# Pairing heads across two groups so that landmark products run in 64-row, 32-column array tiles

## The chip, the cores and the metric

The kernel runs on one core of a Trainium2 chip. The metric is the device time of one execution in microseconds (us). Times come from repeated runs; engine rows come from one profiled execution. PE is the matmul engine (PEld its weight loads), DVE the vector engine, ACT the scalar engine, POOL the GpSimd engine, SP the queue that issues all the DMAs of this kernel.

## The reference

Eight batches of Nystrom attention (8 heads, 576 tokens, 64 dimensions, 32 landmarks) are followed by a two-dimensional Fourier mixing, a layer norm and a two-layer MLP (512 to 2048 to 512):

```python
q_lm = q.reshape(B, H, m, S // m, D).mean(axis=3)     # m = 32, S // m = 18
k_lm = k.reshape(B, H, m, S // m, D).mean(axis=3)
A, Bm, C = sm(q, k_lm), sm(q_lm, k_lm), sm(q_lm, k)   # softmax of scaled products
Z = Bm.T / (norm_1(Bm) * norm_inf(Bm) + 1e-06)        # per head
for _ in range(6):
    Z = 2 * Z - Z @ Bm @ Z
x = A @ Z @ C @ v                                     # heads side by side: (B, S, 512)
u = x + real(fft(fft(x, axis=1), axis=2))
un = (u - mean(u)) / sqrt(var(u) + 1e-06)
out = u + relu(un @ w_ch1) @ w_ch2
```

## The kernel before

The program is fully unrolled. Three threads of Python generators emit it: `attention` (one `tokens` and one `landmarks` generator for each batch, and `mix` behind them), `weights` (decodes and splits the MLP weights into a high and a low f16 part) and `mlp`. A planner (`run`, `Timed`, `till`) keeps a model time `now` and a model arrival for each tile, and so writes out the order of the PE instructions by hand. PE runs in exactly that order. The order of the other engines is chosen by the compiler's scheduler from its own priorities, except for instructions marked `keep_in_program_order`. While PE has nothing planned early on, the planner fills in dummy matmuls on `idle` and `ones16`.

A batch has eight heads in two groups of four. `load` (L360) brings, for each group g, one 128-row tile of k and one of q with two head pairs side by side: the rows are the 2 x 64 dimensions of the heads of a pair. It issues two DMAs of 128 rows for each group on SP, and then the v tile. `tokens` (L382) sums 18 neighbouring tokens into landmarks (`lm`, DVE reduces), takes the absolute sums of q (`Abs` on ACT with an accumulator, `am`) for a power-of-two scale, spreads the q landmarks of the two heads of a pair into a block-diagonal tile `qbd` with a mask (four DVE instructions), makes a masked split copy `kbd` of the k landmarks, and splits q into f16 parts (`qm`, `qr`). The scale of k goes through a matmul with ones (`bound`, tile `kb`). Then come the scores of A in three rounds u (two of 24 matmuls for the first 512 tokens, and one of 12 for the remaining 64), their softmax, their transposes (`AT`), and sums and differences of token tiles (`F1`, `F2`, `Fh`) which feed the token Fourier transform (`CS`).

`landmarks` (L536) computes B from `qbd` and `lm` (4 matmuls, K=128 rows, 64 columns), and C from `qbd` and the k tile (8 matmuls of 288 columns, all fp32). An fp32 matmul stands in the trace as two MATMUL rows. B goes through a softmax chain on DVE and ACT (`Bd`, `nrm`, `BT`); C through a maximum (`cmx`) and an exponential. Six steps of the iteration follow (`RE`, `E`), and the products `Wx`, `Wt`, `WC`. PSUM has eight banks: four for the attention (`at`, in rotation), two for `h`, two for `acc`. In batch 1 `landmarks` waits between B and C until the first MLP chunk is far enough.

`mix` makes the rows `u`. `norm` (L798) normalizes them, two 128-row tiles at a time: in batch 0 mean and variance come from ACT (a `Copy` and a `Square` with accumulators for each tile), in later batches from DVE (`bn_stats`, `bn_aggr`). The first four tiles are transposed on PE, later ones by DMA. `mlp` works on chunks of two tiles: 24 matmuls of 256 columns into `h`, 12 of 512 columns into `acc`, eight times for each chunk. All DVE, ACT and POOL instructions of this kernel pass through `Timed` and stand in the profile as L127; nearly all matmuls as L210, transposes on PE as L215.

Of the kernel before, what the change touches and what calls it, by code (L numbers as in the profile page):

```python
# [41 lines left out]
OFF = 768  # L42

# [61 lines left out]
class Timed:  # L105


    def __init__(self, kernel, engine, fixed, rate, fast):
        self.kernel, self.engine, self.fixed, self.rate, self.fast, self.free = kernel, engine, fixed, rate, fast, 0.0

    def __getattr__(self, name):
        call = getattr(self.engine, name)

        def emit(out, *args, **kw):
# [12 lines left out]
            return call(out, *args, **kw)  # L127
# [4 lines left out]
class Kernel:  # L132
    def __init__(self, ctx, tc, NB, q, k, v, w1, w2, t1, t1t, t2, diag, mask, out):
# [9 lines left out]
        self.V, self.A = Timed(self, nc.vector, 0.07, 1.04e-3, 0.52e-3), Timed(self, nc.scalar, 0.2, 0.83e-3, 0.83e-3)  # L143
# [216 lines left out]
    def load(self, b):  # L360
# [21 lines left out]
    def tokens(self, b, st):  # L382
# [6 lines left out]
        lm = sm.tile([P, 2, 128], F32, name="lm", bufs=1)  # L389
        am = self.small(4, "amax")  # L390
        qbd = sm.tile([P, 4, 64], F32, name="qbd", bufs=1)
        qhs = []
        for g in range(2):
            kf, qf = loads[g][0][:, 0 : 2 * S], loads[g][1][:, 0:NQ]
            first = V.tensor_reduce(lm[:, g, 64:128], kf.rearrange("p (m t) -> p m t", t=18), AX.X, ALU.add)
# [3 lines left out]
            lv = lm[:, g, 0:64].rearrange("p (x o m) -> p x o m", o=2, m=8)  # L399
# [6 lines left out]
            A.activation(qhs[g][:, 0:NQ], qf, AF.Abs, accum_out=am[:, g : g + 1])  # L406
# [5 lines left out]
            yield self.till(qbd)  # L412
        V.tensor_reduce(am[:, 2:4], lm[:, :, 64:128], AX.X, ALU.max, apply_absolute_value=True)
        st["loads"], st["qbd"], st["lm"] = loads, qbd, lm
        self.spawn(self.landmarks(b, st))

        eq, rq = self.power(am[:, 0:2], 2, 2.0**-13, "aq", b == 1)
        kb = self.small(2, "kb", BF16)
        V.tensor_tensor(kb, am[:, 2:4], eq, ALU.mult)
        yield self.till(kb, more=AM)  # L420
        ek, rk = self.bound(kb, 2, 2.0**-13, "ak")
        sc = self.small(4, "sc")
        V.tensor_tensor(sc[:, 0:2], eq, rk, ALU.mult)
        V.tensor_scalar(sc[:, 2:4], ek, 1.0 / 144.0, None, ALU.mult)
# [4 lines left out]
        for h2 in range(2):  # L429
            ms, cols = self.mask2[:, h2 : h2 + 1], slice(32 * h2, 32 * h2 + 32)  # L430
            V.tensor_scalar(
                kbd[..., cols].rearrange("p g y r m -> p (g y r) m"), klm.rearrange("p g y (r m) -> p (g y r) m", r=2),
                ms, None, ALU.mult,
            )
        qm = [h[:, 0:2048].rearrange("p (y r t) -> p y r t", y=2, r=2) for h in qhs]
        qr = [h[:, 2048:2304].rearrange("p (y r t) -> p y r t", y=2, r=2) for h in qhs]
        for g in range(2):
# [6 lines left out]
            if g == 0:  # L444
                yield self.till(qhs[0], kbd)
# [90 lines left out]
    def landmarks(self, b, st):  # L536
# [39 lines left out]
        while b == 1 and self.seconds < NF // 2 - HB:  # L576
            yield 0.5
# [446 lines left out]
```

## Time and profile before

| | |
|---|---|
| median of 3 runs (lowest to highest) | 1018.75 us (1017.17 to 1018.84) |
| profiled execution, its own time | 1018.43 us |
| its span from the first to the last instruction | 1016.6 us |
| PE busy | 969.0 us, 95% |
| DVE busy | 608.2 us, 60% |
| ACT busy | 335.5 us, 33% |
| HBM read, written | 48.02 MB, 9.44 MB |

The span and the execution's own time differ by 1.8 us, which lie outside of the traced instructions. PE busy counts overlapping matmuls once, and a matmul's row is longer than the distance to the next matmul when they are pipelined, so the price of a matmul is read from the distance of starts, not from its row's length.

### The profile page before, as it was taken

To read this page: it belongs to the slowest core of one execution; us is meant where nothing else is said; L and a number is where in the kernel's file an instruction comes from. 1 tells how busy PE (TensorE), PEld (TensorE's weight loads), DVE (VectorE), ACT (ScalarE), POOL (GpSimd) and SP (SyncE) were. 2 spreads that over 40 slices of the span, in tenths; PEclk is the share of its full clock that TensorE was granted. 3 is DMA by queue.
4 is the path that set the end of the run, shared out by engine and by line. 5 is a ranking of instruction groups with operands and counts; after the bars stand their busy time and mean duration, and the time that the engine had idled before them with its cause. 6 is when DMAs were issued, how large, how long until landed. Compare 5 with 4: busy or idle time off the path is not lost.

```text
span 1016.6 us, 20320 instructions
## 1 busy us (share of the span) xinstructions
PE 969.0 (95%) x8407; PEld 673.3 (66%) x8407; DVE 608.2 (60%) x1654; ACT 335.5 (33%) x723; POOL 125.9 (12%) x144
## 2 busy tenths in 40 slices
PE   5776989999999999999999999999999999999998
PEld 3654756667776676666766776667676676666665
DVE  6979797786655855287556855686453834351111
ACT  4658653343223322142233323332212322111110
POOL 0000000013011400024011401122020220110000
PEclk8887999999999999999999999999999999999999
DMA  9863204142312240112402240225020200120000
GB/s 328 254 250 111 83 2 167 22 71 51 148 21 45 43 164 11 43 36 53 161 12 53 50 168 6 58 48 180 1 53 11 58 15 22 22 53 21 1 22 21
DMA packets 97772, 74.63 MB, mean 73 GB/s; under 512 B 68112, under 2 KB 86544, under 8 KB 97552
## 3 DMA queue, kind: packets, MB, share of 16 engines
q1 hardware_dynamic: 97680, 73.34, 24.7%
q8 instruction: 66, 1.08, 0.5%
q14 instruction: 26, 0.21, 0.1%
HBM read 48.02 MB, written 9.44 MB: 57 GB/s over the span
## 4 chain that ended last, share of the span: by engine, by line
PE 82%; DVE 11%; ACT 3%; DMA 2%; issue 1%; POOL 1%; SPq 0%; DVEq 0%; POOLq 0%; ACTq 0%
PE h L210 34%; PE acc L210 34%; PE at L210 13%; DVE w L127 2%; DVE mid L127 1%; ACT mid L127 1%; DMA mid<-mid 1%; DVE lm L127 1%; DVE cmx L127 1%; DVE asum L127 1%; DMA big<-q_dram 1%; DMA big<-k_dram 1%; POOL mid L127 1%; PE at L215 1%; DVE amx L127 0%
## 5 line engine op out<-in xcount | busy, mean ns | idle before, releaser
L210 PE MATMUL h<-unT,w 128*128 128x256 f16 x3456 | 411.2, 273 | 0.0
L210 PEld LDWEIGHTS <-w 128*128 128x128 f16 (+1 forms) x3584 | 346.2, 99 | 73.2 <-issue 3.3
L210 PE MATMUL acc<-w,h 128*128 128x512 f16 x1680 | 394.3, 380 | 0.0
L210 PEld LDWEIGHTS <-h 128*128 128x128 f16 x1680 | 161.8, 98 | 161.9 <-issue 4.4
L127 DVE SCALAR_TENSOR_TENSOR h<-h 128x512 f16<-128x512 f32 x140 | 96.1, 687 | 198.7 <-ACT h L127 198.0
L127 ACT ACTIVATE h<-h 128x512 f16<-128x512 f32 x140 | 83.2, 595 | 308.0 <-PE h L210 295.8
L127 POOL TENSOR_TENSOR r<-ve,mhalf 128x2 f32<-128x2 f32 (+1 forms) x20 | 13.7, 685 | 411.1 <-DVE ve L127 404.1
L127 POOL TENSOR_TENSOR mid<-mid 128x640 f16<-128x640 f32 (+2 forms) x36 | 40.9, 1144 | 114.2 <-ACT mid L127 107.9
L127 DVE TENSOR_TENSOR mid<-mid 128x256 f32<-128x256 f32 (+2 forms) x68 | 45.3, 682 | 13.2 <-DMA mid<-mid 9.4
L127 DVE TENSOR_REDUCE lm<-big 128x32 f32<-128x576 f32 (+1 forms) x48 | 44.2, 946 | 10.2 <-DMA big<-k_dram 9.5
L127 DVE SCALAR_TENSOR_TENSOR u<-at,scw,row 128x128 f32<-128x128 f32 (+3 forms) x120 | 38.6, 389 | 13.8 <-PE at L210 11.8
L210 PEld LDWEIGHTS <-big 128*128 128x128 f16 (+1 forms) x768 | 39.7, 101 | 10.2 <-issue 2.8
L210 PEld LDWEIGHTS <-mid 64*128 64x128 f16 (+1 forms) x624 | 30.0, 96 | 18.8 <-issue 8.6
L127 ACT CAST row<-row 128x512 f16<-128x512 f32 (+1 forms) x40 | 20.7, 551 | 62.7 <-DVE row L127 62.7
L127 DVE SCALAR_TENSOR_TENSOR row<-at,scw,row 128x262 f32<-128x262 f32 (+1 forms) x48 | 21.3, 486 | 28.3 <-ACT row L127 21.4
L127 POOL TENSOR_TENSOR row<-row 128x512 f16<-128x512 f32 (+1 forms) x33 | 34.3, 1055 | 30.7 <-ACT row L127 28.8
L210 PE MATMUL at<-RE,E 128*128 128x96 f32 (+1 forms) x192 | 30.5, 281 | 4.3 <-DVE RE L127 4.3
L127 DVE SCALAR_TENSOR_TENSOR u<-acc,wsc,u 128x512 f32<-128x512 f32 x36 | 26.8, 749 | 12.5 <-PE acc L210 11.8
L210 PEld LDWEIGHTS at<-RE,E 128*128 128x128 f32 x192 | 27.1, 194 | 10.6 <-DVE RE L127 4.4
L210 PE MATMUL at<-mid,big 128*128 128x262 f16 (+1 forms) x288 | 31.8, 279 | 0.0
L127 DVE SCALAR_TENSOR_TENSOR big<-big,aq_r 128x1024 f16<-128x1024 f32 (+1 forms) x32 | 26.8, 868 | 3.9 <-ACT big L127 3.9
L127 ACT CAST mid<-mid 128x512 f16<-128x512 f32 (+1 forms) x28 | 18.1, 671 | 28.2 <-POOL mid L127 20.5
(166 smaller groups left out, 928.6 us busy)
## 6 DMA issues: line engine op xcount, KB each, us to landing
w<-w_dram SPq DMA_DIRECT2D x22, 512.0 KB, 8.7
big<-v_dram SPq DMA_DIRECT2D x16, 640.0 KB, 8.9
big<-q_dram SPq DMA_DIRECT2D x16, 584.0 KB, 6.0
big<-k_dram SPq DMA_DIRECT2D x16, 576.0 KB, 5.0
out_dram<-u SPq DMA_DIRECT2D x36, 256.0 KB, 2.0
big<-w_dram SPq DMA_DIRECT2D x10, 512.0 KB, 6.8
t<-t_dram SPq DMA_DIRECT2D x1, 1048.0 KB, 9.2
unT<-row SPq DMA_TRANSPOSE x64, 2.5
```

The lines of the kernel that those rows point to most:

```text
L127: return call(out, *args, **kw)
L210: self.nc.tensor.matmul(out, a, b, start=start, stop=stop, skip_group_check=True)
L215: self.nc.tensor.transpose(out, a, ident)
```

## The change

Heads are paired across the groups. The tile for e = 0, 1 now holds in its rows 0 to 63 the two heads of pair e of group 0 side by side, and in rows 64 to 127 those of group 1; it is loaded by two DMAs of 64 rows for k and two for q. B and C of one head are then products of 64 rows and 32 output columns, taken straight from `lm` and the k tile; there is no `qbd`. All B and C matmuls of a batch are emitted together into four banks, and B lies in spare columns of two of the C banks. In batch 1 the wait for the MLP stands ahead of both. One scale serves q and one serves k for each row instead of one for each group, so `scr` goes, and `klm` needs one split instead of two. The first two rounds of A now cover two token tiles for all eight heads; the third has 24 matmuls of 32 columns instead of 12 of 64. The sums and differences run on whole 512-column tiles and are emitted after all of the transposes. `mix` indexes `AT` accordingly. The first ten ACT instructions that pass through `Timed` are kept in program order. The first two tiles of batch 0 take their variance from `bn_stats`.

```diff
+PIN = 10
@@ Timed.emit
+            ins = call(out, *args, **kw)
+            if self.pinned > 0:
+                self.kernel.tc.keep_in_program_order(ins)
+                self.pinned -= 1
+            return ins
@@ load
-            gs = slice(2 * g, 2 * g + 2)
-            nc.sync.dma_start(kf[:, 0 : 2 * S].rearrange("p (r t) -> p r t", r=2), self.k[b, :, gs])
-            nc.sync.dma_start(qf[:, 0 : 16 * SEG].rearrange("p (r t) -> p r t", r=2), self.q[b, :, gs])
-            for t in (kf, qf):
+            for t, src, n in ((kf, self.k, S), (qf, self.q, 8 * SEG)):
+                for half in range(2):
+                    nc.sync.dma_start(
+                        t[64 * half : 64 * half + 64, 0 : 2 * n].rearrange("p (o t) -> p o t", o=2),
+                        src[b, :, 2 * half + g].rearrange("(o p) t -> p o t", o=2),
+                    )
@@ tokens
-            for h2 in range(2):
-                ms, cols = self.mask2[:, h2 : h2 + 1], slice(32 * h2, 32 * h2 + 32)
-                V.tensor_scalar(
-                    qbd[:, 2 * g : 2 * g + 2, cols], lm[:, g, 0:64].rearrange("p (r m) -> p r m", r=2), ms, None, ALU.mult
-                )
+    V.tensor_tensor(qs, am[:, 0:1], am[:, 1:2], ALU.add)
+    eq, rq = self.power(qs, 1, 2.0**-13, "aq", b == 1)
-        for g in range(2):
-            split(klm[:, g, 0], klm[:, g, 1], lm[:, g, 64:128], sc[:, g : g + 1])
+        split(*(klm[:, y].rearrange("p e m -> p (e m)") for y in range(2)), lm[:, 1].rearrange("p e m -> p (e m)"), sc[:, 0:1])
-        scr = self.small(1, "scr")
-        for g in range(2):
-            V.tensor_copy(scr[64 * g : 64 * g + 64], sc[64 * g : 64 * g + 64, 2 + g : 3 + g])
...
+                for r in range(4):
+                    for g in range(2):
+                        mm3(ps[64 * g : 64 * g + 64, 32 * r : 32 * r + 32], lambda y: qr[r // 2][:, y, r % 2],
+                            lambda y: kbd[:, y, r // 2, r % 2, 32 * g : 32 * g + 32])
...
+        F1 = [self.mid()[:, 0:512] for _ in range(2)]
+        for x, op in enumerate((ALU.add, ALU.subtract)):
+            V.tensor_tensor(F1[x], aes[0], aes[1], op)
+        for x, op in enumerate((ALU.add, ALU.subtract)):
+            F2 = self.mid()[:, 0:512]
+            for k in range(2):
+                (V if x == 0 else G).tensor_tensor(F2[:, 256 * k : 256 * k + 256], F1[k][:, 0:256], F1[k][:, 256:512], op)
@@ landmarks
-        ps = self.psum()
-        for g in range(2):
-            for pr in range(2):
-                mm(ps[64 * pr : 64 * pr + 64, 32 * g : 32 * g + 32], qbd[:, 2 * g + pr], lm[:, g, 64 + 32 * pr : 96 + 32 * pr])
-        V.tensor_scalar(Bd.rearrange("p g m -> p (g m)"), ps[:, 0:64], 1.0 / 2592.0, None, ALU.mult)
+        while b == 1 and self.seconds < NF // 2 - HB:
+            yield 0.5
+        yield self.till(lm, banks=4)
+        heads = [(slice(64 * g, 64 * g + 64), slice(32 * r, 32 * r + 32), g, r // 2, r % 2) for r in range(4) for g in range(2)]
+        halves = [[self.psum() for g in range(2)] for hf in range(2)]
+        for half, row, g, e, o in heads:
+            mm(halves[0][g][row, 288:320], lm[half, 0, e, 32 * o : 32 * o + 32], lm[half, 1, e, 32 * o : 32 * o + 32], share=0.3)
+        for hf in range(2):
+            for half, row, g, e, o in heads:
+                kv = loads[e][0][half, S * o + 288 * hf : S * o + 288 * hf + 288]
+                mm(halves[hf][g][row, 0:288], lm[half, 0, e, 32 * o : 32 * o + 32], kv, share=0.21)
+        for g in range(2):
+            V.tensor_scalar(Bd[:, g], halves[0][g][:, 288:320], 1.0 / 2592.0, None, ALU.mult)
...
-                ps = self.psum()
-                for pr in range(2):
-                    mm(ps[64 * pr : 64 * pr + 64, 0:288], qbd[:, 2 * g + pr], kv[:, pr, 288 * hf : 288 * hf + 288])
-                V.tensor_reduce(cmx[:, hf : hf + 1], ps[:, 0:288], AX.X, ALU.max)
+                V.tensor_reduce(cmx[:, hf : hf + 1], halves[hf][g][:, 0:288], AX.X, ALU.max)
@@ norm
-        if b == 0:
+        if b == 0 and self.ntile > 0:
```

## Rows read from the trace of the kernel before

**Rows 1.** The page's parts 1 and 2: busy time and share of PE, and PE's busy tenths in 40 slices of 25.4 us.

```profile
span 1016.6 us, 20320 instructions
PE 969.0 (95%) x8407; PEld 673.3 (66%) x8407; DVE 608.2 (60%) x1654; ACT 335.5 (33%) x723; POOL 125.9 (12%) x144
PE   5776989999999999999999999999999999999998
```

**Rows 2.** Busy time of each engine in four stretches. Columns: the stretch, its length, busy us and instructions of PE, PEld, DVE, ACT and POOL, the granted clock as a share of 2.4 GHz, the DMA engines' share, GB/s.

```profile
10.00:20.00 10.00, 3.75 (x20) 1.68 (x20) 8.43 (x33) 4.87 (x13) 0.00 (x0) 0.83 1.10 352
20.00:30.00 10.00, 7.43 (x121) 6.15 (x124) 8.22 (x33) 7.81 (x17) 0.00 (x0) 0.66 1.07 373
80.00:90.00 10.00, 4.71 (x40) 4.04 (x41) 9.25 (x20) 8.20 (x15) 1.13 (x1) 0.59 0.27 93
200.00:1016.00 816.00, 808.64 (x6891) 556.07 (x6889) 443.14 (x1198) 223.70 (x489) 117.25 (x126) 1.00 0.20 54
```

**Rows 3.** PE's own timeline in batch 3: start, length, the group merged from matmuls of one kind, their count.

```profile
313.79 0.86 PE L210 MATMUL at<-mid,big 128*64 128x262 f16 x12
314.58 0.52 PE L210 MATMUL at<-Wx,row 64*64 64x128 f16 x12
...
319.60 2.78 PE L210 MATMUL h<-unT,w 128*128 128x256 f16 x24
322.22 2.75 PE L210 MATMUL acc<-w,h 128*128 128x512 f16 x12
...
326.21 0.43 PE L210 MATMUL at<-lm,qbd 128*64 128x32 f32 x8
326.47 2.36 PE L210 MATMUL at<-big,qbd 128*64 128x288 f32 x16
328.76 1.48 PE L210 MATMUL h<-unT,w 128*128 128x256 f16 x12
...
331.41 0.49 PE L210 MATMUL at<-nrm,ones_bd 128*128 128x128 f32 x2 [0.52 <-ACT mid L127]
...
343.49 1.73 PE L210 MATMUL at<-big,mid 128*32 128x64 f32 x80
345.15 1.27 PE L210 MATMUL at<-kbd,big 128*128 128x64 f16 x36
346.35 1.47 PE L210 MATMUL acc<-w,h 128*128 128x512 f16 x6
```

**Rows 4.** The same view in batch 0: six matmuls that use 64 rows of the array each, alternating between the halves, and PE's next group.

```profile
51.70 0.58 PE L210 MATMUL at<-t1t,row 64*128 64x320 f16 x6
52.21 0.69 PE L210 MATMUL at<-RE,E 128*128 128x96 f32 x4
```

**Rows 5.** DVE instructions grouped by line and form over the whole span: count, busy us, mean ns of one, idle time before them.

```profile
L127 DVE BATCH_NORM_STATS2 bn<-u 128x6 f32<-128x512 f32 x32 | 20.6, 681 | 0.0
L127 DVE TENSOR_SCALAR qbd<-lm,mask 128x64 f32<-128x64 f32 x32 | 6.9, 248 | 0.1
L127 DVE BATCH_NORM_AGGREGATE mv<-bn 128x2 f32<-128x6 f32 x32 | 5.0, 174 | 0.0
```

**Rows 6.** The start of the run in the timeline of all engines. A bracket says how long the engine had been idle, and what ended it.

```profile
1.19 0.42 SPq L368 DMA_DIRECT2D big<-k_dram  x1
...
2.60 0.67 SPq L369 DMA_DIRECT2D big<-q_dram  x1
...
5.78 2.85 DVE L127 TENSOR_REDUCE lm<-big 128x64 f32<-128x1152 f32 x3 [3.07 <-DMA big<-k_dram]
...
10.57 1.41 DVE L127 TENSOR_REDUCE lm<-big 128x32 f32<-128x576 f32 x2
...
12.48 0.31 PE L210 MATMUL at<-lm,qbd 128*64 128x32 f32 x4 [3.04 <-DVE qbd L127]
...
18.60 1.18 ACT L127 ACTIVATE big<-big 128x1168 f16<-128x1168 f32 x1
...
21.75 0.18 PE L210 MATMUL at<-kb,ones 128*128 128x2 bf16 x1 [5.51 <-DVE cr L127]
```

**Rows 7.** DMA issues of the first 30 us: count, KB each, median us from issue to landing.

```profile
big<-q_dram SPq DMA_DIRECT2D x2, 584.0 KB, 6.5
big<-k_dram SPq DMA_DIRECT2D x2, 576.0 KB, 5.5
```

**Rows 8.** The timeline around the first norm and up to the first MLP matmul.

```profile
75.04 1.90 DVE L127 SCALAR_TENSOR_TENSOR u<-at,scw,row 128x256 f32<-128x256 f32 x6
...
80.36 0.70 ACT L127 ACTIVATE row<-u,nm 128x512 f32<-128x512 f32 x1
...
81.19 0.17 DVE L127 TENSOR_SCALAR ve<-rt 128x2 f32<-128x2 f32 x1
...
85.29 1.94 PE L215 MATMUL at<-ident,row 128*128 128x128 f32 x8 [5.68 <-DVE row L127]
...
91.88 4.09 PE L210 MATMUL h<-unT,w 128*128 128x256 f16 x36
```

**Rows 9.** The timeline at B of batch 1.

```profile
131.36 0.31 PE L210 MATMUL at<-lm,qbd 128*64 128x32 f32 x4
...
133.36 0.41 DVE L127 TENSOR_SCALAR qbd<-lm,mask 128x64 f32<-128x64 f32 x2
...
133.83 0.31 PE L210 MATMUL at<-lm,qbd 128*64 128x32 f32 x4 [2.16 <-DVE qbd L127]
```

More of the change, by code (lines that the diff above doesn't have):

```diff
@@ L105, with __init__ @@
 class Timed:
-    def __init__(self, kernel, engine, fixed, rate, fast):
+    def __init__(self, kernel, engine, fixed, rate, fast, pinned=0):
         self.kernel, self.engine, self.fixed, self.rate, self.fast, self.free = kernel, engine, fixed, rate, fast, 0.0
+        self.pinned = pinned
     def __getattr__(self, name):
@@ L388, in tokens @@
         NQ = 16 * SEG
-        lm = sm.tile([P, 2, 128], F32, name="lm", bufs=1)
-        am = self.small(4, "amax")
-        qbd = sm.tile([P, 4, 64], F32, name="qbd", bufs=1)
+        lm = sm.tile([P, 2, 2, 64], F32, name="lm", bufs=1)
+        am = self.small(2, "amax")
         qhs = []
-        for g in range(2):
-            kf, qf = loads[g][0][:, 0 : 2 * S], loads[g][1][:, 0:NQ]
-            first = V.tensor_reduce(lm[:, g, 64:128], kf.rearrange("p (m t) -> p m t", t=18), AX.X, ALU.add)
+        for e in range(2):
+            kf, qf = loads[e][0][:, 0 : 2 * S], loads[e][1][:, 0:NQ]
+            first = V.tensor_reduce(lm[:, 1, e], kf.rearrange("p (m t) -> p m t", t=18), AX.X, ALU.add)
             if b == 1:
                 self.tc.keep_in_program_order(first)
-            lv = lm[:, g, 0:64].rearrange("p (x o m) -> p x o m", o=2, m=8)
+            lv = lm[:, 0, e].rearrange("p (x o m) -> p x o m", o=2, m=8)
             qv = qf.rearrange("p (x o t) -> p x o t", o=2, t=2 * SEG)
@@ L414, in tokens @@
-        st["loads"], st["qbd"], st["lm"] = loads, qbd, lm
+            A.activation(qhs[e][:, 0:NQ], qf, AF.Abs, accum_out=am[:, e : e + 1])
+            yield self.till(lm)
+        kb = self.small(2, "kb", BF16)
+        km, qs = self.small(1, "kmax"), self.small(1, "qsum")
+        V.tensor_reduce(km, lm[:, 1].rearrange("p e m -> p (e m)"), AX.X, ALU.max, apply_absolute_value=True)
+        st["loads"], st["lm"] = loads, lm
         self.spawn(self.landmarks(b, st))
-        eq, rq = self.power(am[:, 0:2], 2, 2.0**-13, "aq", b == 1)
@@ L429, in tokens @@
-        for h2 in range(2):
-            ms, cols = self.mask2[:, h2 : h2 + 1], slice(32 * h2, 32 * h2 + 32)
             V.tensor_scalar(
-                kbd[..., cols].rearrange("p g y r m -> p (g y r) m"), klm.rearrange("p g y (r m) -> p (g y r) m", r=2),
-                ms, None, ALU.mult,
+                kbd[..., 32 * g : 32 * g + 32].rearrange("p y e r m -> p (y e r) m"), klm.rearrange("p y e (r m) -> p (y e r) m", r=2),
+                self.mask2[:, g : g + 1], None, ALU.mult,
             )
@@ L539, in landmarks @@
         V, A = self.V, self.A
-        loads, qbd, lm = st["loads"], st["qbd"], st["lm"]
+        loads, lm = st["loads"], st["lm"]
         m4g = lambda m: self.mask4.unsqueeze(1).unsqueeze(3).broadcast_to([P, 2, 4, m])
@@ L574, in landmarks @@
         V.tensor_tensor(BTd, wide(BT, 32), m4g(32), ALU.mult)
-        while b == 1 and self.seconds < NF // 2 - HB:
-            yield 0.5
         for g in range(2):
-            kv = loads[g][0][:, 0 : 2 * S].rearrange("p (r t) -> p r t", r=2)
             Ce = self.mid()
@@ L596, in landmarks @@
                 A.activation(
[L597 removed]
+                    Ce[:, 288 * hf : 288 * hf + 288], halves[hf][g][:, 0:288], AF.Exp, bias=cb, scale=1.0 / 144.0,
                     accum_out=csum[:, hf : hf + 1],
```

73 lines of the change are left out of this document (26 added, 47 removed).

## The prediction

> **What bounds the kernel now.** I read the page first, for the shares of the engines and the slices. PE is busy in 95% of the span, and after the fourth slice its digit is 9 almost to the end [rows 1]. The windows then split the run in two: from 200 us on PE is busy for 808.64 of 816 us, and DVE for little more than half [rows 2]. In that part time falls only when PE has less to stream, or stalls less. The first hundred microseconds are different. There PE is busy 3.75 and 4.71 us in two of the 10 us stretches shown, and DVE 8.22 to 9.25 us in all three [rows 2]. In that part a microsecond is won when DVE idles less or when a chain of small steps ends sooner. So the change is priced twice: as PE time in batches 1 to 7, and as chain time at the start.
>
> I then read PE's timeline of one batch in that second part for prices by distance of starts [rows 3], the timeline of all engines at the start [rows 6], around the first norm [rows 8], and at batch 1, whose B still holds PE up [rows 9].
>
> **B and C, the main term.** B and C of a batch run from 326.21 to 328.76, 2.55 us: 0.26 for 8 rows of B and 2.29 for 16 rows of C [rows 3]. The tiles of 64 columns already run two at once: 12 such f16 matmuls of 262 columns take 0.79 us, 66 ns each, where full-width ones of 256 columns take 2.62/24 = 109 ns each [rows 3]. C's 16 rows are then 8 pairs of 286 ns. After the change there are 32 rows of C and 16 of B, each in one of eight tiles (two row halves, four column quarters). How many of the eight run at once decides everything, and no row shows both directions together. The rows show each alone: 64-row tiles go two at once (6 matmuls of 320 columns in 0.51 us, 85 ns each, against 109 ns for 256 columns) [rows 4], and 32-column tiles go four at once (80 fp32 rows of 64 columns in 1.66 us, 21 ns each, where the 36 f16 ones of 64 columns behind them, most of full width, take 1.20/36 = 33 ns) [rows 3]. If the directions combine, C is 32/8 = 4 rounds of 286 ns, 1.14 us, and B two rounds of the 0.26/4 = 65 ns that one took before. With some skew between eight tiles I take 1.4 us. That saves 1.1 us in each batch. The bounds: 1.45 us saved, if a round is as fast as the stream of `h` allows (109 ns for 256 columns; 288 columns at half that pace are 245 ns, four of them and B 1.1 us); nothing saved if four run at once (8 rounds are 2.29 us again); and a loss of 2.5 us if only two do (16 rounds are 4.58 us, and B 0.5). I take eight, because both directions are seen alone and the tiles of a pair write to different banks. In batches 1 to 7 this is 7 x 1.1 = 7.7 us.
>
> Bd can be read only when C's first half, in the same bank, is written too. That delays the B chain by about half of C, 0.6 us. In batches 2 to 7 it lies under MLP matmuls, which fill PE from 328.76 on [rows 3]; where that cover is missing, in batch 0, it costs its 0.6 us, against up to 1.1 that C saves there, and I count the two as 0.
>
> **A, the third round.** The 36 matmuls took 1.20 us with their switches of tile shape [rows 3]. The third round has 12 more. At 33 ns they would add 0.4 us; if all 24 go at the 21 ns that the column tiles show, it adds 24 x 0.021 - 12 x 0.033 = 0.1 us. The halves alternate every three matmuls, which is nearer to the tiled row, so I take 0.1: +0.7 us over seven batches, at most +2.8.
>
> **DVE and ACT work.** Four `qbd` masks (4 x 248 ns) go, 1.0 us in each batch [rows 5], and two `scr` copies and one `klm` split besides. One `Bd` and one addition of sums come, and two wide first differences replace four narrow ones; I let these small ones cancel. After 200 us DVE has room and all of it is worth 0. At the start it is 1.0 us less on an engine that is over 80% busy, but the first norm puts 2 x (681 + 174) = 1.7 us onto it [rows 5]. The rest, 0.7 us, fits into DVE's idle 1.57 and 0.75 us of the stretches shown [rows 2]; I take 0, and uncovered it is +0.7.
>
> The sums and differences now wait for both rounds of A. The transform behind them needed both before, too: 0. The intermediate tiles remain ten for seven buffers. An allocation that comes later would be covered by MLP work; uncovered it is one DVE step, 0.7 us.
>
> **Loads.** SP issues eight DMAs for k and q instead of four, at 0.42 us or a little more each: some 1.7 us more on SP in each batch [rows 6]. Behind them stand v and the weight pieces in batch 0, and the transposes of tokens and of `unT` later. In batch 0, transfers set the pace, not issues: the second q tile is issued at 2.60 and consumed at 10.57 [rows 6], and k and q land 5.5 and 6.5 us after issue [rows 7]. Later loads come far ahead of use. So 0, if 64-row transfers run at the rate of 128-row ones; no row shows one. The four tiles hold 2.32 MB, 6.6 us at the 352 GB/s of [rows 2]. If half the rows meant half the rate, the last tile would come up to 6.6 us late. I take +1 at the start, nearer to the shared stream of full rate, and keep +6.6. The Trainium skill (SBUF — State Buffer, Door 1: the DMA port swizzle) speaks against the change: 64 neighbouring rows reach half of the ports, so a transfer to them gets half the bandwidth. By that rule the last tile would be the 6.6 us late; by the stream in the row, nothing.
>
> **The first ten ACT instructions.** The first `Abs` of q runs at 18.60 and the other behind it, though the second q tile was there at 10.57 when DVE read it; and PE stands 5.51 us in front of the `kb` matmul, which needs them [rows 6]. In program order the `Abs` are the first two ACT instructions of all. They end near 12, and `kb` can follow C near 14 to 15 instead of 21.75. Queued behind `kb` on PE are the row sums of B, the transposes of C and the scores of A. What is late next is DVE: all of this work was spread over 12 to 30, where DVE idled 1.57 + 1.78 = 3.3 us [rows 2]. I take that idle time as the gain, 3 us; the bounds are 7 (all of the earlier `kb`) and a loss of 3 (a pinned exponential that waits for C's maximum keeps the weight decoding behind it from starting).
>
> **The first norm.** Its `u` is ready at 75.04 + 1.90 = 76.94 and `ve` starts at 81.19, 4.25 us later, while PE idles 5.68 us ahead of the transposes at 85.29 [rows 8]. On DVE the same takes 1.7 us plus one or two queued weight steps of 0.75, say 3.2. Gain 1; bounds 0 and 2.5.
>
> **Batch 1.** PE waits 2.16 us for the second `qbd` [rows 9]. Without masks it may start at about 132.8, when the reduces ahead of 133.36 end: gain 1.0; bounds 0 and 2.2, since the moved wait puts B later in PE's order as well.
>
> **The sum.** Start: +1 - 3 - 1 = -3 us. Batch 1: -1. Batches 1 to 7: -7.7 + 0.7 = -7. Together -11 against the profiled 1018.43 (span 1016.6 and 1.8 around it): 1007.4. The median of the runs is 0.3 above the profiled execution, so I say 1007.6.
>
> **The rivals.**
> 1. Two tiles at once. The 64-row and the 32-column split do not combine, and each fp32 row has to wait for the row of its own tile just ahead. For it: no row shows eight tiles. Against it: four quarters already overlap although the two rows of each fp32 matmul stand next to each other. C and B take 5.1 us, +2.5 x 7 = +17.6, and the time is 1018.4 + 17.6 + 0.7 - 4 = 1033. It turns into a slower kernel once C and B take over 3.0 us: the 0.47 x 7 lost would eat the other 3.3.
> 2. Four at once: the main term is 0, and 1018.4 + 0.7 - 4 = 1015.
> 3. Half-rate loads. A 64-row load writes at half the rate, and the last q tile comes 6.6 us late instead of 1: 1007.6 + 5.6 = 1013. For it: DMA is full from 10 to 30 [rows 2], so anything late there stays late. Against it: the other half follows at once on the same queue. This is what the page's port rule would do here.
> 4. A pinned instruction blocks ACT, and the start is +3 instead of -3: 1013.6. For it: the exponentials need a chain through PE and DVE, and weight decoding stands behind them. Against it: DVE has its own work meanwhile.
> 5. The banks. B and C take all four attention banks at once; PE already waits 0.52 us for an exponential to free one at 331.41 [rows 3]. With C ending 1.1 us earlier and the exponentials no sooner, that wait grows by up to the whole gain. 0.5 to 1 us x 7: about 1013. Against it: other work can be planned in between.
>
> **How the numbers follow.** Forecast 0.60, half-rate loads 0.08, ACT blocked 0.06, banks 0.10, four at once 0.08, two at once 0.08. The likeliest case alone ranges from 1001 (7 x 1.45 for C, two thirds of the start's 9.5 us of bounds, 2 at batch 1) to 1013. The range 1000 to 1018 takes in cases 2 to 5 and leaves out case 1 and the far ends. A change of 0.2%, 2 us, is about what a measurement of this kernel can tell from none. Faster: nearly all of the forecast and of banks and most of cases 2 to 4, 0.77. Slower: case 1 and the bad tails of 3 and 4, 0.14. Same: 0.09.
>
> **What would show it.** C's 32 rows in about 1.1 to 1.3 us with eight starts close together, and an `h` matmul 1.4 us after the first B; both `Abs` before 13 and `kb` near 15; q's second tile consumed near 10.6, or as late as 17 if the loads are slow; the first `h` matmul, now at 91.88 [rows 8], near 89; no wait of 2 us at batch 1. The prediction is wrong if C's starts come in pairs, if a new wait stands at `nrm` or `kb` in each batch, or if `h` starts later than before.

## The result, and the profile after

The changed kernel is slower. Its median is 1026.38 us (1024.81 to 1029.31) against 1018.80 for the kernel before on the same chip: a ratio of 1.0077, with a 95% interval of 1.0052 to 1.0101. The forecast was 1007.6. The profiled execution took 1024.81 us with a span of 1023.0, 6.4 more than before. Executions of one kernel differ by up to 1.1%, and the longer ones show the lower mean granted clock (in experiment 7, five took 1014.2 to 1015.1 us at 0.979 to 0.981 and seven 1020.3 to 1025.1 us at 0.968 to 0.975), so verdicts rest on medians and intervals, and a trace stands for one execution.

The page of the kernel after, parts 1 and 2, answers [rows 1]. PE is busy for 4.4 us less, and the span is longer all the same.

```profile
span 1023.0 us, 20956 instructions
PE 964.6 (94%) x8714; PEld 671.8 (66%) x8714; DVE 600.6 (59%) x1600; ACT 332.2 (32%) x707; POOL 125.8 (12%) x144
PE   4867888999999999999999999999999999999998
```

The stretches of [rows 2] in the kernel after (columns as there). PE is busier from 80 to 90 us, since `h` begins earlier, and idles more after 200 us: 10.4 us in 822, where it was 7.4 in 816.

```profile
10.00:20.00 10.00, 2.85 (x49) 1.11 (x49) 6.09 (x17) 4.74 (x11) 0.00 (x0) 0.67 1.09 309
20.00:30.00 10.00, 6.10 (x30) 4.91 (x31) 7.68 (x38) 6.44 (x15) 0.00 (x0) 0.50 1.06 372
80.00:90.00 10.00, 9.18 (x85) 7.65 (x86) 8.58 (x20) 8.20 (x15) 0.00 (x0) 0.74 0.17 54
200.00:1022.00 822.00, 811.56 (x7154) 558.71 (x7152) 436.55 (x1157) 223.53 (x484) 117.30 (x126) 1.00 0.23 53
```

**The main term is there.** PE's timeline of batch 4 in the kernel after answers [rows 3]. B and C begin at 455.84 and MLP work follows at 457.04, so both cost 1.20 us. The last 29 of C's 32 rows take 1.16 us from the first start to the last end. Single rows start in four groups of eight, at 455.93, 456.17, 456.41 and 456.66, the eight of a group within 0.05 us: all eight tiles run at once, in four rounds of 0.24 us.

```profile
455.84 0.27 PE L217 MATMUL at<-lm 64*32 64x32 f32 x13
...
455.95 1.16 PE L217 MATMUL at<-big,lm 64*32 64x288 f32 x29
457.04 2.12 PE L217 MATMUL acc<-w,h 128*128 128x512 f16 x9
```

In the kernel before, B of batch 4 began at 450.39 and the MLP at 452.72, 2.33 us. So 1.13 us are won, and as much in batches 2, 5 and 6. The Trainium skill (TensorEngine Tiling (Array Packing), Available Configurations) lists 64x32 as a mode of eight tiles; this trace agrees, with the 1.20 us.

**The first loss: batch 1.** PE's timeline there in the kernel after, which answers [rows 9], then one row of DVE and one of ACT. All 48 matmul rows of B and C are out by 137.1. Then PE stands for 3.31 us in front of `kb`. What `kb` reads was written by DVE at 137.43, so the 3 us behind that are the wait for a bank: C fills all four, the first exponential that empties one starts at 139.80, and `kb` starts at 140.44. Behind `kb` in PE's order stand 15 `acc` matmuls that need none of this.

```profile
134.29 0.27 PE L217 MATMUL at<-lm 64*32 64x32 f32 x8
135.90 0.23 PE L217 MATMUL at<-lm 64*32 64x32 f32 x4 [1.34 <-DVE lm L130]
...
135.98 1.15 PE L217 MATMUL at<-big,lm 64*32 64x288 f32 x28
140.44 0.16 PE L217 MATMUL at<-kb,ones 128*128 128x1 bf16 x1 [3.31 <-ACT mid L130]
140.47 4.73 PE L217 MATMUL acc<-w,h 128*128 128x512 f16 x15
...
157.42 0.65 PE L222 MATMUL at<-ident,mid 128*128 128x128 f32 x4 [1.91 <-POOL mid L130]
```

```profile
137.27 0.16 DVE L130 TENSOR_TENSOR kb<-kmax,aq_e 128x1 bf16<-128x1 f32 x1
```

```profile
139.80 0.50 ACT L130 ACTIVATE mid<-at,cb 128x288 f32<-128x288 f32 x1 [0.90 <-DVE cb L130]
```

The stall costs more than its length. Busy time by short stretches of the kernel after (columns as in [rows 2]): PE did nothing from 138 to 140, and the clock it was granted then fell to 0.50 (1.2 GHz) for 2 us and was 0.70 on the mean for 2 more, with PE working again. That is 1.0 + 0.6 = 1.6 us of work at full clock.

```profile
138.00:140.00 2.00, 0.00 (x0) 0.00 (x0) 2.00 (x12) 0.57 (x3) 0.00 (x0) 0.95 0.00 0
140.00:142.00 2.00, 1.56 (x5) 0.58 (x5) 2.00 (x13) 2.00 (x8) 0.00 (x0) 0.50 0.00 0
142.00:144.00 2.00, 2.00 (x8) 0.79 (x7) 2.00 (x11) 1.55 (x4) 0.00 (x0) 0.70 0.00 0
```

**The second loss: batches 2 to 7.** PE's waits after 200 us (total, times, longest): first the kernel before, 4.0 us in all, then after, 7.6 us. The waits for RE, the iteration's matrix, have tripled. Here, too, clock goes with a wait: behind waits of 1.06 and 0.50 us for RE, up to 480.54 in batch 4, the clock granted from 482 to 484 us was 0.50, and with its flanks that is 1.7 us of work. The two for `u` are in batches 3 and 7, where C's second half finds a bank not yet read.

```profile
PE at L210 <- DVE RE L127: 2.0, 2, 1.6
PE at L210 <- ACT mid L127: 1.0, 2, 0.5
PE at L210 <- DVE nrm L127: 0.7, 1, 0.7
PE at L210 <- DVE kbd L127: 0.3, 1, 0.3
```

```profile
PE at L217 <- DVE RE L130: 6.0, 7, 1.3
PE at L217 <- DVE u L130: 1.6, 2, 0.8
```

One of those waits, in batch 3 of the kernel after, over POOL, DVE and PE. DVE's sum needs POOL's normalization of the second round, waits 1.96 us at the head of DVE's queue, and RE stands behind it.

```profile
354.21 1.05 POOL L130 TENSOR_TENSOR mid<-mid,asum 128x512 f32<-128x512 f32 x1
355.30 0.87 DVE L130 TENSOR_TENSOR mid<-mid 128x512 f32<-128x512 f32 x1 [1.96 <-POOL mid L130]
356.09 0.33 DVE L130 TENSOR_SCALAR RE<-at,cr,ci 128x64 f32<-128x64 f32 x1
356.48 0.46 PE L217 MATMUL at<-RE,E 128*128 128x96 f32 x2 [1.01 <-DVE RE L130]
```

What made the sum late is to be seen on PE. These are the scores of A in batch 2, of the kernel before and of the kernel after. Before, the first round goes out at 230.89 and the other two at 237.24, with MLP work between; after, all three go out in one block of 72. The first round used to need the first q tile alone; with heads paired across groups it needs both, and so all rounds become ready together (experiments 7 and 10 set them apart again).

```profile
230.89 0.86 PE L210 MATMUL at<-kbd,big 128*128 128x64 f16 x24
237.24 1.27 PE L210 MATMUL at<-kbd,big 128*128 128x64 f16 x36
```

```profile
228.04 2.05 PE L217 MATMUL at<-kbd,big 128*128 128x64 f16 x72
```

**The start.** ACT, DVE and PE of the kernel after, for [rows 6] and [rows 8]. The `Abs` run at 10.21 and 13.78, not at 18.60. But the second q tile comes at 13.79; the load of ACT's function table, 1.28 us, ran at 0.73 before and now stands behind the wait for q; and `kb` is at 22.03, because DVE takes `qsum` only behind a weight step that waited for its DMA. The first `h` comes at 85.63, 6.25 us earlier than before. Little of that lasts: the first `acc` matmul of chunk 0 is at 120.97, where it was at 119.49, with PE waiting 0.82 us for DVE's `wm` and 0.61 for ACT's `w` just ahead, steps of the weight decoding.

```profile
8.91 1.28 ACT L130 ACT_TABLE_LOAD   x1 [8.91 <-DMA big<-q_dram]
10.21 1.18 ACT L130 ACTIVATE big<-big 128x1168 f16<-128x1168 f32 x1
13.78 1.18 ACT L130 ACTIVATE big<-big 128x1168 f16<-128x1168 f32 x1 [2.31 <-DMA big<-q_dram]
```

```profile
13.79 1.41 DVE L130 TENSOR_REDUCE lm<-big 128x32 f32<-128x576 f32 x2 [0.66 <-DMA big<-q_dram]
20.18 0.43 DVE L130 TENSOR_SCALAR w<-w 128x512 int32<-128x512 int32 x1 [1.32 <-DMA w<-w_dram]
20.59 0.15 DVE L130 TENSOR_TENSOR qsum<-amax 128x1 f32<-128x1 f32 x1
```

```profile
22.03 0.19 PE L217 MATMUL at<-kb,ones 128*128 128x1 bf16 x1 [4.19 <-DVE kb L130]
...
85.63 0.82 PE L217 MATMUL h<-unT,w 128*128 128x256 f16 x6
```

What the DMA engines moved in the first 30 us, 40 slices of 0.75 us, kernel after and kernel before. With 64-row transfers the stream is at 212 to 276 GB/s for 14 slices; before, it was at 330 to 415 in the same place, behind a first slice of 264.

```profile
GB/s 0 0 4 46 276 261 243 255 212 252 228 243 249 214 252 224 233 235 337 350 348 348 350 347 350 348 358 341 352 350 333 384 453 404 426 411 347 349 355 347
```

```profile
GB/s 0 0 16 104 264 394 330 342 414 381 415 403 379 385 371 347 351 347 348 350 347 348 344 345 357 341 383 458 428 414 380 356 350 348 355 354 348 345 350 348
```

### The profile page after: what moved, and what is told of

The parts are those of the page before. It is cut to its first block, busy times and chain, and to the rows that moved or that the text cites. A ratio compares the mean times of both kernels' runs of the same rounds, so it can differ in the third digit from the quotient of the medians.

```text
span 1023.0 us, 20956 instructions
## 1 busy us (share of the span) xinstructions
PE 964.6 (94%) x8714; PEld 671.8 (66%) x8714; DVE 600.6 (59%) x1600; ACT 332.2 (32%) x707; POOL 125.8 (12%) x144
## 4 chain that ended last, share of the span: by engine, by line
PE 65%; DVE 11%; issue 11%; DMA 6%; POOL 3%; ACT 2%; SPq 2%; POOLq 0%; DVEq 0%; ACTq 0%
PE h L217 28%; PE acc L217 27%; PE at L217 10%; DVE mid L130 2%; DVE w L130 2%; POOL mid L130 2%; DMA big<-q_dram 2%; DMA w<-w_dram 2%; DMA mid<-mid 1%; DVE u L130 1%; DMA diag<-ny_dram 1%; DVE row L130 1%; SPq L641 1%; DVE lm L130 1%; DVE h L130 1%
## 5 line engine op out<-in xcount | busy, mean ns | idle before, releaser
L130 DVE TENSOR_TENSOR mid<-mid 128x256 f32<-128x256 f32 (+3 forms) x52 | 39.7, 797 | 16.7 <-POOL mid L130 9.0
L217 PE MATMUL at<-RE,E 128*128 128x96 f32 (+1 forms) x192 | 31.4, 284 | 10.5 <-DVE RE L130 10.3
L130 ACT ACTIVATE w<-w,wsc 128x512 f16<-128x512 f32 x32 | 22.6, 719 | 17.2 <-DVE w L130 9.3
L217 PE MATMUL acc<-idle,ones 128*128 128x256 bf16 x144 | 26.8, 329 | 1.5 <-DVE idle L175 1.5
```

The source lines that it names most:

```text
L130: ins = call(out, *args, **kw)
L217: self.nc.tensor.matmul(out, a, b, start=start, stop=stop, skip_group_check=True)
```

## The experiments

Ratios are against the kernel before on the same chip, in the same series. The changed kernel's is 1.0077. The diffs are shortened; `...` and `@@` stand for lines left out.

**1. Loads of 128 rows.**

```diff
-                for half in range(2):
-                    nc.sync.dma_start(t[64 * half : 64 * half + 64, ...], src[b, :, 2 * half + g]...)
+                nc.sync.dma_start(t[:, 0 : 2 * n].rearrange("p (o t) -> p o t", o=2), src[b, :, gs])
@@ layout
-    heads = sum(GROUPS, [])
+    heads = [GROUPS[g][i] for i in range(4) for g in range(2)]
```

> The changed kernel, with each k and q tile brought by one DMA of 128 rows again; the heads are permuted in DRAM instead, so everything behind the loads stays as changed. Theory L (64-row transfers share the queue at 215 to 275 GB/s instead of 330 and more, and the last q tile is 3.2 us late): over 330 GB/s again between 5 and 10 us, the last q tile read near 10.6 to 11.0 instead of 13.8, and the end 2 to 3 us earlier, about 1023.5 to 1024.5 against the changed kernel's 1026.4. Theory W (the start is paced by the weights, whose decoding stands behind the ten pinned ACT instructions): the tile comes as early as under L, but the end moves by less than 1 us, 1025.5 to 1026.5.

Measured: 1024.92 us, ratio 1.0054 (1.0037 to 1.0072). Behind a first slice of 307, the stream is back at 347 to 429 GB/s, and DVE reads the last q tile at 10.32, 3.5 us earlier (DVE of this kernel; the row below it is ACT's):

```profile
10.32 1.40 DVE L130 TENSOR_REDUCE lm<-big 128x32 f32<-128x576 f32 x2
```

```profile
0.73 1.28 ACT L130 ACT_TABLE_LOAD   x1 [0.73 <-PEq L1012]
```

The end moves by 1.5 us on the medians and 2.3 on the ratios, between the two theories, and the intervals overlap. So half-row loads are slow, as theory L has it, but not all of that reaches the end: in this trace PE waits 3.58 us for `wm`, where it waits 0.82 in the kernel after, and `acc` of chunk 0 begins at 123.55. The table load is back at 0.73, with the ten instructions still pinned, and `kb` comes at 18.39. So it was not the pin alone that put the load behind the wait; only the pinned kernels with two half-row loads for a tile show that.

**2. Nothing pinned.**

```diff
-PIN = 10
+PIN = 0
```

> The changed kernel with no ACT instruction pinned. Theory W: the first weight pieces are decoded earlier again (Prelu from about 12 to 14 us, the fourth piece near 28 instead of 40.5), the last split of the first weight ends near 99 to 103 instead of 115.2, chunk 0 of the second MLP layer ends near 161 to 165 instead of 170.6, and the kernel takes about 1020 to 1022. Theory L: the late loads set the pace whatever the order on ACT is; the first h comes at 88 to 92 instead of 85.6, the end of chunk 0 stays within 2 us of 170.6, and the time within 1.5 us of 1026.4.

Measured: 1023.03 us, ratio 1.0036 (1.0022 to 1.0051). The pinned order costs 3.4 us by the medians and 4.2 by the ratios; the intervals lie side by side, so the sign is settled and the size roughly. Theory L, by which the time would stay, is missed too: the first `h` comes at 80.70, 4.9 us earlier. What the pin held up is to be seen on ACT, for one step at least. The second decoding step of the weights (`row<-w`) runs at 17.20 here, in the first row, and at 21.67 in the kernel after, in the second, where it stands in program order behind the four exponentials of C.

```profile
17.20 0.69 ACT L130 ACTIVATE row<-w 128x512 f32<-128x512 f32 x1 [0.82 <-DMA w<-w_dram]
```

```profile
21.67 0.66 ACT L130 ACTIVATE row<-w 128x512 f32<-128x512 f32 x1
```

Chunk 0 of the second layer still ends at 170.8 (170.6 in the kernel after), so theory W, by which it would end at 161 to 165, falls, and so does any account by which the start alone lost the 8 us. The two traces differ in clock: from 117 to 200 us it was 0.94 here and 0.98 there. By an estimate from these, 0.04 x 83 = 3.3 us, chunk 0 would have ended near 167.5 at the same clock, which is still too late for theory W.

**3. A's rounds over tiles 0, 2 and 1, 3.** Each first difference needs one round again.

```diff
-                        at = 128 * (2 * u + j)
+                        at = 128 * (u + 2 * j)
@@ in the loop over u, behind AT
+                F1.append(self.mid()[:, 0:512])
+                for x, op in enumerate((ALU.add, ALU.subtract)):
+                    V.tensor_tensor(F1[u][:, 256 * x : 256 * x + 256], ae[:, 0:256], ae[:, 256:512], op)
@@ behind the loop, in place of F1 and the halves of F2
+            (V if x == 0 else G).tensor_tensor(F2, F1[0], F1[1], op)
```

> The changed kernel, with A's first round over token tiles 0 and 2 and the second over 1 and 3. So the first differences again need one round each, and only the second ones need both; the work is the same. Theory Q (in batches 2 to 7 the first differences stand at the head of DVE's queue until POOL has normalized the second round, and the iteration's RE behind them holds PE up): PE's waits for DVE RE after 200 us fall from 6.0 us to about 2, as in the kernel before, and the time falls by about 4, to 1022.4. Rival M (the wait only moves: the second differences, or the banks that C now takes all four of, stop PE instead): the RE waits fall, but other waits for DVE or ACT after 200 us grow by as much, and the time stays within 1 us of 1026.4.

Measured: 1033.15 us, ratio 1.013 (1.011 to 1.015): both theories missed. The waits for RE after 200 us did not fall but grew to 10.3. The narrow sums of this kernel hardly wait for POOL now (0.7 us in 24 of them); four of them run as a block, 0.91 us each, and RE stands behind them all the same. The row below them is one sum of this form in the kernel before, at a time when POOL has nothing to do.

```profile
236.46 3.63 DVE L130 TENSOR_TENSOR mid<-mid 128x256 f32<-128x256 f32 x4
240.02 0.33 DVE L130 TENSOR_SCALAR RE<-at,cr,ci 128x64 f32<-128x64 f32 x1
```

```profile
240.73 0.41 DVE L127 TENSOR_TENSOR mid<-mid 128x256 f32<-128x256 f32 x1
```

Behind the two longest of these waits (3.44 us up to 240.41, 3.69 up to 586.45) the granted clock was 0.50 from 241 to 247 and from 586 to 592 us; PE worked for 10.1 us of that, so in this trace some 5 us went with the clock. So the dependence on both rounds was not the cause; that the rounds come as a block was still a possible one.

**4. The first norm as before.**

```diff
-        if b == 0 and self.ntile > 0:
+        if b == 0:
```

> The changed kernel, with mean and variance of the first two tiles from ACT's Copy and Square again. If the norm change is worth what was forecast for it, the first h comes about 1 us later than 85.6 and the time is up to 1 us longer (1026.4 to 1027.4). If it shortens the chain by the three us that the ACT passes and their round trips take, the first h comes near 88 to 89; and if the weights pace the MLP behind it (theory W), the end still moves by less than 1 us.

Measured: 1028.74 us, ratio 1.009 (1.0075 to 1.0105). The first `h` comes at 90.70, 5.1 us later, more than either case allowed; of that 2.4 us show in the medians and 1.3 in the ratios, whose intervals overlap. So a loss from the norm change is unlikely, and a small gain is not clear of noise.

**5. The kernel before, with the sums in one go.**

```diff
-            if u < 2:
-                F1, F2 = ...
+            if u == 2 or b > 1:
+                continue
+            sums(u)
+        for u in range(2 if b > 1 else 0):
+            sums(u)
```

> The kernel before, with one part of the change: in batches 2 to 7 the sums and differences are emitted in one go behind all three rounds of A, not behind each round. They still need one round each, and the work is the same. Theory Q (a bunch of sums stands in DVE's queue ahead of the iteration's RE and E): PE's waits for DVE RE after 200 us grow from 2.0 us to 5 to 8, and the time from 1018.8 to 1022 to 1025. Rival S (where the sums stand matters little; the waits of the changed kernel come from the shorter C and the other order around it): the waits stay under 3.5 us and the time within 1.5 us of 1018.8.

Measured: 1018.14 us, ratio 0.9999 (0.9991 to 1.0008). Where the sums are emitted does nothing as long as the rounds are apart. Theory Q in this form falls.

**6. Normalization on DVE.**

```diff
-            (self.G if b > 0 else V).tensor_tensor(av, av, bc(asum), ALU.mult)
+            V.tensor_tensor(av, av, bc(asum), ALU.mult)
```

> The changed kernel, with the softmax normalization of A on DVE instead of POOL in batches 1 to 7. Theory P (the sums are late because POOL normalizes both rounds behind one another and writes token parts between, and DVE's own 512-column sums run at 0.87 to 1.64 us beside POOL against 0.67 alone): PE's waits for RE after 200 us fall from 6.0 to 3 or less, the 1.9 us ahead of batch 1's transposes go, and the time falls by 4 to 6, to 1020.5 to 1022.5. Rival: the 1.6 us of normalization that DVE gets in each batch stand ahead of RE just as the sums did; the waits stay at 5 or more, and the time within 1.5 us of 1026.4.

Measured: 1022.42 us, ratio 1.0038 (1.0025 to 1.0052), 4 us less; the RE waits are 3.7 us. POOL is part of the chain, as theory P has it, though 3.7 is more than its 3. The 3.3 us at `kb` are still there, and the 1.9 us ahead of batch 1's transposes did not go: PE waits there for DVE, 1.5 and 1.3 us.

**7. The third experiment's kernel, its rounds apart.**

```diff
-            yield self.till(*qhs)
+            yield self.till(*qhs, *(aes if b >= 2 else []))
```

> The third experiment's kernel (rounds over tiles 0, 2 and 1, 3), where in batches 2 to 7 PE's order places the second and third round of A only when the round ahead of it is planned to be normalized; before the change the first round needed one q tile and the second the other, which had kept them apart. Theory Q: the four narrow first differences no longer stand in one block of 3.6 us in DVE's queue; PE's waits for RE after 200 us fall from the 10 us of the third experiment to 3 or less, and the time from 1033 to 1021 to 1024. If spacing the rounds does nothing, the time stays above 1029 and another cause than the bunch is behind the third experiment's loss.

Measured: 1020.88 us (1014.23 to 1025.10), ratio 1.0011 (0.9987 to 1.0035), 12 us below the third experiment; its slowest execution is faster than the fastest there (1028.52). No wait for RE is left after 200 us; 5.3 us of others are, 2.1 of them for `u` at `acc`.

**8. `kb` after a free bank, in batch 1 alone.**

```diff
         yield self.till(kb, more=AM)
+        if b == 1:
+            yield self.till(banks=1)
```

> The changed kernel, where in batch 1 alone the matmul of the k scale (kb) is placed in PE's order only when one of the four banks that B and C hold is planned to be free, so that MLP matmuls go ahead of it. Theory B (the banks: C in all four at once holds kb up): the 3.31 us wait at kb falls below 0.5 and the end comes 2 to 3 us earlier, 1023.5 to 1024.5. Rival: what kb feeds (the masked k copy and the scores of A) is late by the same amount and PE waits there or at the transposes instead; the end moves by less than 1 us.

Measured: 1017.61 us, ratio 1.0002 (0.9989 to 1.0015). That is 8.8 us by the medians and 7.6 by the ratios from one matmul's place and the order that follows from it, more than either theory allowed. PE's timeline of this kernel in batch 1: the `acc` matmuls go first, and `kb` waits for nothing.

```profile
136.41 1.15 PE L217 MATMUL at<-big,lm 64*32 64x288 f32 x28
137.49 2.98 PE L217 MATMUL acc<-w,h 128*128 128x512 f16 x13
...
143.32 0.17 PE L217 MATMUL at<-kb,ones 128*128 128x1 bf16 x1
```

From 117 to 200 us PE's waits add up to 12.8 us in the kernel after and to 7.3 here: the 1.91 us ahead of the transposes is gone too, since PE now has `h` and `acc` matmuls to put in between. And the granted clock over these 83 us is 1.00, where it was 0.98, 1.7 us. Together that is 7.2 of the 7.6 us between the two spans. Behind 200 us two differences nearly cancel: PE waits 1.2 us more here (8.8), and the loss of clock at 482 us, 1.7 us, is missing.

**9. The same edit in the kernel before.**

```diff
         yield self.till(kb, more=AM)
+        if b == 1:
+            yield self.till(banks=1)
```

> The kernel before, with the edit of the eighth experiment: in batch 1 kb is placed in PE's order only when an attention bank is planned to be free. Theory B (the wait at kb became this dear only because the change fills all four banks at once): before, PE waits 1.40 us at kb [rows of the chain in batch 1], so at most 1.4 to 2 us are won, 1016.5 to 1018.8. Rival: kb's place was as bad for the kernel before, and the edit is worth some 8 us there too, near 1010; then the eighth experiment says nothing of the change.

Measured: 1019.87 us, ratio 1.0013 (1.0003 to 1.0024): no gain. The 1.40 us at `kb` go, and `nrm` waits 2.47 instead of 0.53. So the place of `kb` became dear only with the change.

**10. `kb` after a free bank, and the change's own rounds apart.** The edits of 8 and 7 without that of 3.

```diff
+        if b == 1:
+            yield self.till(banks=1)
...
-            yield self.till(*qhs)
+            yield self.till(*qhs, *(aes if b >= 2 else []))
```

> The eighth experiment's kernel (kb after a free bank) and, as in the seventh, A's second and third round placed apart in batches 2 to 7, but with the change's own rounds and sums. Theory Q2 (rounds that follow one another at once put POOL's two normalizations and DVE's sums in one block ahead of RE): the 7.2 us of RE waits after 200 us fall to 3 or less, and the time from 1017.6 to 1012 to 1014. Rival: the waits only go to where the later rounds are needed (the transforms or the products behind them); the RE waits fall, others after 200 us grow, and the time stays within 1.5 us of 1017.6.

Measured: 1011.57 us, ratio 0.9932 (0.9919 to 0.9945). The rounds in PE's timeline of batch 2 are apart, and of the 8.8 us that PE waited after 200 us in experiment 8, 2.3 are left, none for RE. The change's sums still need both rounds here.

```profile
232.02 0.86 PE L217 MATMUL at<-kbd,big 128*128 128x64 f16 x24
239.69 0.87 PE L217 MATMUL at<-kbd,big 128*128 128x64 f16 x24
```

```profile
PE at L217 <- DVE u L130: 1.6, 2, 0.8
PE at L217 <- DVE Wx L130: 0.7, 2, 0.4
```

The 512-column sums themselves show it: DVE's groups from 200 to 1000 us of the kernel after, then of this one (busy, mean ns, idle just before them). They are as long in both; what goes is 9.0 us in which they stood at the head of the queue, waiting for POOL.

```profile
L130 DVE TENSOR_TENSOR mid<-mid 128x512 f32<-128x512 f32 x12 | 13.3, 1122 | 9.0 <-POOL mid L130 9.0
```

```profile
L130 DVE TENSOR_TENSOR mid<-mid 128x512 f32<-128x512 f32 x12 | 13.6, 1159 | 0.0
```

**11. Experiments 3, 7 and 8 together.**

```diff
+            yield self.till(banks=1)
...
-            yield self.till(*qhs)
+            yield self.till(*qhs, *(aes if b >= 2 else []))
...
-                        at = 128 * (2 * u + j)
+                        at = 128 * (u + 2 * j)
```

> The seventh and the eighth experiment's edits together: rounds over tiles 0, 2 and 1, 3, placed apart, and kb after a free bank. If the two losses (batch 1, and the block of sums) are independent, the gains of 8.8 and 5.5 us add up: 1012. If rounds over tiles 0 and 2 are no better than the change's own once they are apart, this kernel stands within 1.5 us of the tenth experiment's.

Measured: 1010.11 us, ratio 0.9912 (0.9899 to 0.9926). The two gains add up, to the 1012 expected and a little more. Rounds over tiles 0 and 2 bring at most 0.2% beside experiment 10, and the intervals overlap.

**12. The same, with 128-row loads and nothing pinned.**

```diff
-PIN = 10
+PIN = 0
...
+                nc.sync.dma_start(t[:, 0 : 2 * n].rearrange("p (o t) -> p o t", o=2), src[b, :, gs])
```

> The eleventh experiment's kernel, with loads of 128 rows and no pinned ACT instruction, as in the first two experiments. If the parts are independent, their 1.5 and 3.3 us add to the rest: 1007 to 1008, which is where the forecast had put the change, and faster than the kernel before by about 1%. If the start is covered once batch 1 is mended (the weights pace it), the two are worth less than 1.5 us together, and the time is near the eleventh's.

Measured: 1008.59 us, ratio 0.9916 (0.9899 to 0.9934). Faster than both kernels, by 0.8% and 1.6%, but by ratio no faster than experiment 11. The first `h` is at 77.40 in this kernel and `acc` of chunk 0 begins at 117.97, against 120.91 in experiment 11; but from 117 to 200 us PE waits 3.0 us for RE in one place, where it waits 1.3 in experiment 11, and the clock granted there was 0.96 in this trace and 1.00 in that one, 3.3 us. The profiled span is 2.6 us shorter (1005.7 against 1008.3), so not all of the start's gain is lost in these two executions; over the runs the two edits are worth 1.5 us by the medians and nothing by the ratios, where experiments 1 and 2 found 4.9 to 6.5 us for them one by one. Why is not shown.

## Why the prediction was wrong

The sum had -11 us, and the change took +7.6. Three steps failed: batch 1's -1, the rounds of A, which no term priced (the sums behind them stood at 0), and the start's -3. In their place the runs showed 7.6 us at `kb` in batch 1, 7 us from rounds that leave as one block, and an `acc` that begins 1.5 us later. The term for B and C held in the main.

**C and B: the mechanism was right, the size in two batches not.** Eight tiles at once, 1.13 us saved in batches 2, 4, 5 and 6, where 1.1 was said. That it came out so closely is partly luck: the step took batch 3's 2.55 us as the price before, where these four show 2.33, and 1.4 as the price after, where they show 1.20, and the two errors cancel. Against that stand batches 3 and 7: 331.71 to 334.44, 2.73 us, where it was 2.55, with 0.78 us of waiting for a bank whose reader, DVE's `u`, waited for an output DMA. In batches 2 to 7 that makes 4 x 1.13 - 2 x 0.2 = 4.1 us, of the 6.6 that were counted for them.

**The third round: right.** Three rounds take 230.02 - 228.04 = 1.98 us where they took 0.70 + 1.20 = 1.90: the +0.1 that was taken.

**Batch 1: wrong, and the largest miss.** The step said -1. B came at 134.29 instead of 131.36, for the reason the bound named (the wait for the MLP now stands ahead of it), PE still waited 1.34 us for `lm`, and `kb` behind C met four full banks. That is rival 5, the banks. Its mechanism was right, but it was spread over seven batches at 0.5 to 1 us each. In batches 2 to 7 MLP work is planned between C and `kb` (457.04 to 460.96 in batch 4), so it costs nothing there; in batch 1 nothing is, and experiment 8 prices it at 7.6 us by the ratios: 3.31 of wait, the clock behind it, and the transposes that came late in turn. The wait in the row is less than half of the price.

**"The sums and differences now wait for both rounds of A ... 0": the step failed, but not by what it says.** Experiments 5 and 10 show that emitting the sums last, and needing both rounds, costs nothing when the rounds are apart. What no step priced is one line above: A's first round now waits for both q tiles. All rounds then leave PE as one block, POOL's two normalizations follow one another, and DVE's sums sit in a queue ahead of RE. Experiment 10 against 8: 0.70% of the time by the ratios, 7 us (6.0 by the medians).

**DVE and ACT work after 200 us, "all of it is worth 0": wrong in its reason.** What the removed masks are worth by themselves was not tested; the reason given, that DVE has room, does not hold. DVE is busy for about half of that part, but PE's order is fixed, so DVE's order decides even so. A share of busy time says nothing of what stands behind a waiting instruction.

**Loads: +1 was near.** The stream fell to about 240 GB/s from about 380, not to half, and the last tile came 3.2 us later (13.79 against 10.57), between +1 and the +6.6 of the half rate. Experiment 1 finds 1.5 to 2.3 us at the end, with overlapping intervals. By the port count of the Trainium skill (SBUF — State Buffer, Door 1: the DMA port swizzle), 8 of 16, the rate would be half; the trace shows 0.6 to 0.7 of the rate before, nearer to what the same section measured for 1 MiB, 196 GB/s on 64 rows against 328 on 128.

**The first ten ACT instructions: wrong sign.** -3 was said. `Abs` came early, but `kb` did not (22.03 against 21.75): the second q tile and the table load were late, and DVE's queue held `qsum` up. And a weight step was held up as rival 4 had it, by pinned exponentials that wait for C's maximum (21.67 against 17.20 in experiment 2). Experiment 2 has 3.4 to 4.2 us of loss, at the bound or past it; how much of that is this step was not tested.

**First norm: right as far as the runs can tell.** -1 was said; experiment 4 has 1.3 to 2.4, not clear of noise.

**The balance.** From 117 to 200 us PE's waits grow from 6.5 to 12.8 us, after 200 us from 4.0 to 7.6; `acc` of chunk 0 begins 1.5 us later (120.97 against 119.49), and 1.4 of the 12.8 us lie ahead of that begin and are in the 1.5 already. B and C stream for 8.7 us in batches 2 to 7 instead of 14.4 (the 1.6 us of waits for `u` left out), and A takes 0.5 more. The granted clock from 117 to 200 us is 0.98 in both; the 1.7 us of clock at 482 us are in the kernel after alone. 4.9 + 3.6 + 1.5 + 1.7 - 5.7 + 0.5 = 6.5, where the spans differ by 6.4. With the two losses mended (experiments 10 to 12, the last two with further edits) the time is 1008.6 to 1011.6, 1 to 4 us above the sum's 1007.6; in experiment 10, which has the change's own start, the 3 us of the start are still missing. (The sum's own last step is 0.1 off: 1007.4 and 0.3 make 1007.7.)

## What to carry to other kernels

When an operand is regrouped, list what each consumer now needs that it did not need before: the gain on PE here was real, and half of what ate it came about because one line came to wait for two tiles instead of one, and three rounds that had been apart became a block. When an instruction that takes all buffers of a pool stands in a hand-written order, look at what comes next from the same pool and put independent work between them, in each batch anew. The price of a stall in such an order is not its length in a trace, since it also delays what stands behind it and can lower the clock.

## What the runs showed of the hardware

- Eight fp32 tiles of 64 rows and 32 columns run at once: 32 rows of C with 288 columns and 16 of B take 1.20 us, C's rows in four rounds of eight that start 0.24 us apart.
- PE's granted clock fell to 1.2 GHz behind a stretch of 3.3 us in which PE did nothing and was back at 1.00 from 144 us on, with PE at work. The kernel of experiment 8, without that stretch, shows 1.00 from 117 to 200 us.
- Four DVE sums in a row beside a working POOL take 0.91 us each, where the same form took 0.41 with POOL idle. The Trainium skill (Trainium Architecture — The Big Picture, What this means for kernel authors) has the two engines lock each other out of a shared port; the two rows agree with it and do not prove it.
- ACT's table load, 1.28 us, ran at 0.73 in the kernel before and in experiments 1, 2 and 12, and only at 8.9 to 9.2 us, behind the wait for q, in the kernels that pin `Abs` first and bring its tile by two loads. Pinned with one load a tile (experiment 1) it kept its early place; what makes the difference was not tested further.
